# A gated delta rule with a rational-function layer: queries transposed on TensorE instead of through DRAM

## The chip, the core and the metric

The kernel runs on one core of a Trainium2 chip. The metric is the device time of one execution in microseconds. The engines are called as in the profile: PE (TensorE; PEld is its weight load), DVE (VectorE), ACT (ScalarE), POOL (GpSimd) and SP (SyncE, which here only issues transfers). All names of lines (L250 and so on) are those of the kernel before.

## What is computed

The reference has two stages. The first is a delta-rule attention over 4 batches of 8 heads, 768 steps and head size 48; the second a layer on each of the 3072 tokens (384 wide, 2048 hidden) whose activation is a rational function.

```python
k_n = k / (norm(k) + 1e-06)
for t in range(S):
    kt, vt, bt = k_n[:, :, t], v[:, :, t], beta[:, :, t, None]
    y[:, :, t] = einsum('bhd,bhde->bhe', q[:, :, t], state)
    v_old = einsum('bhde,bhd->bhe', state, kt)
    state = state + bt * einsum('bhd,bhe->bhde', kt, vt - v_old)
h = x @ w_in                       # x: y with the heads side by side
P = a[0] + a[1]*h + a[2]*h**2 + a[3]*h**3
Q = 1.0 + abs(b[0])*abs(h) + abs(b[1])*h**2
return (P / (Q + 1e-6)) @ w_out
```

All arrays are 32-bit floats. The kernel multiplies on PE in 16 bits: each operand is split into a high and a low 16-bit part, and three products (high-high, low-high, high-low) are summed in PSUM.

## The kernel before

**Chunks and units.** The 768 steps are cut into 12 chunks of 64. A chunk's tile has 128 partitions: 64 steps of two batches. In a chunk the recurrence is solved as a triangular system, so that it becomes matrix products. The layer runs in units: a unit is one of the 8 slices of the hidden size for the 256 tokens of one chunk, 96 units in all. A unit goes through `hidden` (the products with w_in, L851), `numerator` (L868 to L879), `quotient` (L886 to L898) and `accumulate` (the products with w_out, L913). In the numerator ACT's L868 and L870 come first and DVE's L871, L873 and L875 take their results together with PSUM. In the quotient DVE's L892 or L890, L893 and L897 work on operands that all lie in SBUF, and POOL makes the low part of the result at L898 (and, for some units, L879 and L895).

**How the two are interleaved.** A prologue (the string `ORDER`) loads and converts the weights (L382 to L394) and runs the first chunks' attention. After that, beside each unit of chunk c, one slice j of the attention's stages is issued: `back` for chunk c+1, `middle` for c+2, `front` for c+3 and `ahead` for c+4. Some stages are given a higher priority. A scheduler fixes the order of the instructions on each engine before the run; engines then work in that order and wait on one another by semaphores. Nearly all transfers are issued on SP's queue, also in a fixed order, so a transfer that waits holds back those behind it.

**The queries.** `load` (L112) fetches a chunk's queries in four transfers into one buffer, at the end of `ahead`. In `front`, slice 2, `scales` takes the sum of squares of the queries on ACT (L258), finds a power of two as scale by two small products on PE, and copies it out at L696 (tile sc). Then `queries_transposed` (L704) does this:

- POOL multiplies the queries by the scale in place (L261).
- `transposed` (L517) splits them on POOL into a high part (L242) and a low part (L248), both in the tile kn. That tile exists once and is also used for the keys in `keys_normalized`.
- Two transfers take kn to DRAM (L528, xdq).
- One transposing transfer brings the result back to SBUF as tq (L545). For chunk 0 only, PE transposes the 16-bit parts instead (L538) and ACT copies them out of PSUM (L540); its transfers to DRAM are issued all the same.

The tile tq has the head size on its partitions, two batches above each other with a pad from 48 to 64. It is read in `query_products` (L719), slice 3 of `front`, by the products pm (L470), which DVE masks at L725, and later in `diagonals` by the transfers to qbd (L502), which are needed for the chunk's outputs.

**The helpers.** `split16` (L239) is used everywhere for a split: by default ACT makes the high part (L244 without a scale, L246 with one) and DVE the low part (L248 without, L250 with a scale).

**PSUM.** The pool `ps_f` has one buffer of two banks (tag "a"). The products of `front` (pg, pm), the scale's two small products, `off_blocks` (pe) and, from chunk 3 on, the tokens' transposes (px, L819) take turns in it.

Of the kernel before, what the change touches and what calls it, by code (L numbers as in the profile page):

```python
# [10 lines left out]
F16 = mybir.dt.float16  # L11
F32 = mybir.dt.float32
# [26 lines left out]
def kernel(  # L39
# [12 lines left out]
    nc = tc.nc  # L52

    B, H, S, D = q.shape
    DM, DFF = moe_w_in.shape
    P = 128
    C = 64
    DP = 64
    NB = C // 16
    NCH = S // C  # L60
    NPAIR = B // 2
# [4 lines left out]
    HG = 2  # L66
# [39 lines left out]


    SRC = {"k": k, "q": q, "v": v}
    LD_BUFS = {"k": 1, "q": 1, "v": 2}
    loaded = {}  # L110

    def load(nm, c):  # L112
        t = sb.tile([P, NPAIR * H, D], F32, tag="ld" + nm, name=f"{nm}_{c}", bufs=LD_BUFS[nm])
        with behind(nm, c):
            for b in range(2):
                sl, src = slice(b * C, (b + 1) * C), SRC[nm][:, :, c * C : (c + 1) * C]
                if nm == "v":
                    nc.sync.dma_start(out=t[sl], in_=src[2 * b : 2 * b + 2].rearrange("p h t d -> t (p h) d"))
                else:
                    for i in range(2):  # L120
                        nc.sync.dma_start(out=t[sl, i * H : (i + 1) * H], in_=src[2 * i + b].rearrange("h t d -> t h d"))
        loaded[nm, c] = t


    identf = cpool.tile([P, P], F32, name="identf")
    make_identity(nc, identf)
# [130 lines left out]
    def sum_squares(dst, src, junk):  # L257
        nc.scalar.activation(junk, src, AF.Square, accum_out=dst)  # L258

    def scaled(x, scale):  # L260
        nc.gpsimd.tensor_scalar(x, x, scale, 0.0, op0=ALU.mult, op1=ALU.add)  # L261
# [255 lines left out]
    def transposed(x, src, nm, soon):  # L517


        split16(  # L520
            [x[:, i, :, :, :D].rearrange("p h b d -> p b h d") for i in range(2)],
            src.rearrange("p (b h) d -> p b h d", b=2),
            eng=nc.gpsimd,
            hi=nc.gpsimd,
        )
        xd = dpool.tile([NPAIR, 2, NH, C, HG, 2, DP], F16, tag="xd" + nm[0], name=f"xd{nm}", bufs=4 if nm[0] == "k" else 2)
        for p in PAIRS:
            nc.sync.dma_start(  # L528
                out=xd[p].rearrange("i n t a b d -> t (i n) (a b d)"),
                in_=x[p * C : (p + 1) * C].rearrange("t i (n a) b d -> t (i n) (a b d)", n=NH),  # L530
            )
        t = sb.tile([P, NPAIR, 2, NH, C, HG], F16, tag="tt", name="t" + nm)
        if soon:
            pts = ps_f.tile([P, 2, H, P], F16, tag="a", name=f"pt{nm}")
            for i in range(2):
                pt = pts[:, i]
                for h in range(H):
                    nc.tensor.transpose(pt[:, h], x[:, i, h].rearrange("p b d -> p (b d)"), ident16)  # L538
                for p in PAIRS:
                    nc.scalar.copy(  # L540
                        t[:, p, i].rearrange("x n t a -> x n a t"),
                        pt[:, :, p * C : (p + 1) * C].rearrange("x (n a) t -> x n a t", a=HG),
                    )
            return t, xd
        nc.sync.dma_start(  # L545
            out=t.rearrange("x p i n t a -> x (p i n t a)"),
            in_=xd.rearrange("p i n t a b d -> (p i n t a) (b d)"),
            transpose=True,
        )
        return t, xd  # L550
# [127 lines left out]
    def scales(c):  # L678

        qt, vs = loaded.pop(("q", c)), loaded.pop(("v", c))  # L680
        fs = sb.tile([P, 2], F32, tag="fs", name=f"fs_{c}")
        for i, t in enumerate((qt, vs)):
            junk = sb.tile([P, HP, D], F32, tag="fq", name=f"sq{i}_{c}", bufs=1)
            sum_squares(fs[:, i : i + 1], t, junk)
        if "v" in fmax:
            nc.gpsimd.tensor_scalar(fs[:, 1:2], fs[:, 1:2], fmax["v"], 1.0, op0=ALU.max, op1=ALU.mult)
        fmax["v"] = fs[:, 1:2]
        kq = sb.tile([P, 2], F32, tag="kq", name=f"kq_{c}")
        hot = sb.tile([P, 2], BF16, tag="hq", name=f"hq_{c}")
        key_of(kq, total(fs, 2, f"q_{c}"))  # L690
        found(hot, kq)
        pl = ps_f.tile([P, NPAIR * 512], F32, tag="a", name=f"pl_{c}")
        looked_up(pl[:, 0:2], hot[:, 0:1], t_qv[:, 0:2])
        looked_up(pl[:, 2:5], hot[:, 1:2], t_qv[:, 2:5])
        sc = sb.tile([P, 6], F32, tag="sc", name=f"sc_{c}", bufs=4)
        nc.scalar.copy(sc[:, 0:5], pl[:, 0:5])  # L696
        nc.scalar.activation(sc[:, 5:6], sc[:, 1:2], AF.Copy, scale=sc[:, 3:4])
        d = info[c]
        d["sq"], d["sv"], d["isv"], d["ss"], d["iy"] = (sc[:, i : i + 1] for i in (0, 2, 3, 4, 5))
        d["qt"], d["vs"] = qt, vs  # L700
        if c == 0:
            scaled(vs, d["sv"])

    def queries_transposed(c):  # L704
        d = info[c]
        qt = d.pop("qt")
        scaled(qt, d["sq"])
        d["tq"] = transposed(kn_b, qt, f"q_{c}", c == 0)[0]

    def diagonals(c):  # L710
        d = info[c]
# [379 lines left out]
```

## Time and profile before

| | before |
|---|---|
| median of 3 runs | 859.67 us (859.34 to 860.39) |
| the profiled execution's own time | 859.42 us |
| its span, first to last instruction | 857.2 us |
| mean granted TensorE clock | 0.886 |
| HBM read, written | 40.47 MB, 26.23 MB |

The profile shows one execution. Its rows give, for a group of instructions, the line, engine and operation, what it writes and reads ("out<-in" by the program's names), shapes and count, then busy time in us and the mean of one in ns, and after the second bar the idle time of the engine just before them and what ended it. A row of waits ("POOL x <- DMA y: 23.0, 7, 5.2") gives the us in total, the number of times and the longest. A row of the chain of waits gives start and duration in us. In the rows of one line or tile, three numbers with strokes are the shortest, the median and the longest duration in ns.

### The profile page before, as it was taken

The page shows a single profiled execution, that of the slowest core. Times are in us where ns is not written, and L with a number is a line of the kernel's source. Part 1 is how long each engine was busy: PE and PEld are TensorE (multiplying, and loading weights), DVE is VectorE, ACT ScalarE, POOL GpSimd, SP SyncE. Part 2 cuts the span into 40 slices and gives each one's busy share as a digit, 9 for nine tenths or more (in the row PEclk, how much of TensorE's full clock was granted, in tenths as well). Part 3 has the DMA queues.
Part 4 walks back from the last instruction along what each step waited for, and adds up shares of the span by engine and source line. Part 5 has one row for each costly group of instructions (what it writes and reads, how often), then busy time and mean ns, then how long its engine had stood idle before and what let it go on. Part 6 is the DMA issues. An engine that isn't in the chain of part 4 may idle for free.

```text
span 857.2 us, 22995 instructions
## 1 busy us (share of the span) xinstructions
PE 622.0 (73%) x9290; PEld 492.0 (57%) x9290; DVE 760.8 (89%) x1312; ACT 544.9 (64%) x980; POOL 482.7 (56%) x452
## 2 busy tenths in 40 slices
PE   0220344766878688878798697995987989999895
PEld 0220344546666475666586585774775767777663
DVE  5998799697989969989989968999789999898996
ACT  4766656645666465677586574766566766677774
POOL 7655666355326437646736864766665635454532
PEclk9755555897988989989999899998989999999999
DMA  8996868898787875965997988598778672500000
GB/s 235 247 205 132 191 160 152 152 159 152 141 142 130 154 147 89 176 116 104 186 151 132 151 137 173 90 167 150 123 151 153 94 151 47 102 2 20 1 20 19
DMA packets 466506, 111.46 MB, mean 130 GB/s; under 512 B 431328, under 2 KB 463072, under 8 KB 466400
## 3 DMA queue, kind: packets, MB, share of 16 engines
q1 hardware_dynamic: 464224, 108.83, 67.8%
q8 instruction: 73, 1.20, 0.6%
q10 hardware_dynamic: 2176, 1.17, 0.5%
q14 instruction: 33, 0.27, 0.1%
HBM read 40.47 MB, written 26.23 MB: 78 GB/s over the span
## 4 chain that ended last, share of the span: by engine, by line
DVE 40%; DMA 16%; PE 14%; ACT 9%; issue 9%; SPq 7%; POOL 4%; POOLq 0%; ACTq 0%; DVEq 0%
PE ph L851 4%; PE po L913 4%; DVE mw L893 4%; DVE mw L873 3%; DVE mu L871 3%; DVE mg L892 3%; DVE mu L897 3%; DVE w_out L394 3%; DVE pr L636 2%; DVE mu L875 2%; DMA gd<-g 2%; DMA gb<-gd 2%; SPq L676 2%; POOL mg L898 2%; DMA wc<-img 1%
## 5 line engine op out<-in xcount | busy, mean ns | idle before, releaser
L913 PE MATMUL po<-w_out,mg 128*128 128x384 f16 x1152 | 224.9, 341 | 50.5 <-POOL mg L898 43.0
L851 PE MATMUL ph<-xT,w_in 128*128 128x256 f16 x1728 | 216.6, 278 | 13.1 <-DVE mu L875 11.4
L898 POOL TENSOR_TENSOR mg<-mu,mr 128x512 f16<-128x512 f32 x96 | 134.1, 1398 | 115.0 <-DVE mu L897 85.3
L851 PEld LDWEIGHTS <-w_in 128*128 128x128 f16 x1728 | 169.2, 100 | 45.5 <-issue 12.5
L913 PEld LDWEIGHTS <-mg 128*128 128x128 f16 x1152 | 110.2, 101 | 126.5 <-POOL mg L898 51.3
L868 ACT ACTIVATE mu<-ph,coef,msc 128x512 f32<-128x512 f32 x96 | 74.0, 771 | 45.5 <-POOL mg L898 31.0
L874 ACT ACTIVATE mw<-mw 128x512 f32<-128x512 f32 x96 | 60.3, 628 | 64.4 <-DVE mw L873 64.1
L893 DVE SCALAR_TENSOR_TENSOR mw<-mw,msc,mg 128x512 f32<-128x512 f32 x96 | 96.1, 1002 | 0.5
L470 PEld LDWEIGHTS <-kbd 128*128 128x128 f16 x1680 | 61.9, 105 | 36.4 <-issue 27.8
L871 DVE TENSOR_TENSOR mu<-ph,mu 128x512 f32<-128x512 f32 x96 | 65.4, 681 | 19.1 <-ACT mr L870 16.5
L875 DVE SCALAR_TENSOR_TENSOR mu<-mu,msc,ph 128x512 f32<-128x512 f32 x96 | 70.7, 736 | 0.0
L873 DVE SCALAR_TENSOR_TENSOR mw<-mr,msc,ph 128x512 f32<-128x512 f32 x96 | 70.5, 735 | 0.0
L886 ACT ACTIVATE mr<-mw,msc 128x512 f32<-128x512 f32 x96 | 69.2, 720 | 1.5
L895 POOL TENSOR_TENSOR mu<-mu,mw 128x512 f32<-128x512 f32 x36 | 48.7, 1353 | 32.8 <-DVE mw L893 29.1
L870 ACT ACTIVATE mr<-ph,msc 128x512 f32<-128x512 f32 x96 | 65.3, 680 | 0.0
L470 PE MATMUL pu<-z,ebd 128*128 128x48 f16 x1728 | 53.3, 187 | 15.7 <-DVE z L250 14.2
L470 PEld LDWEIGHTS <-ebd 128*128 128x128 f16 x1728 | 52.6, 99 | 19.5 <-issue 16.8
L887 ACT ACTIVATE mr<-mr 128x512 f32<-128x512 f32 x96 | 60.3, 628 | 1.4
L892 DVE SCALAR_TENSOR_TENSOR mg<-mu,msc,mr 128x512 f16<-128x512 f32 x60 | 56.9, 949 | 4.3 <-ACT mr L887 4.3
L879 POOL TENSOR_SCALAR mu<-mu,msc 128x512 f32<-128x512 f32 x36 | 34.2, 949 | 38.8 <-DVE mu L875 38.7
L897 DVE SCALAR_TENSOR_TENSOR mu<-mu,msc,mw 128x512 f32<-128x512 f32 x60 | 54.3, 907 | 0.4
L470 PEld LDWEIGHTS <-wbd 128*128 128x128 f16 x1152 | 35.1, 99 | 33.9 <-issue 30.4
(211 smaller groups left out, 1247.8 us busy)
## 6 DMA issues: line engine op xcount, KB each, us to landing
wsi<-in_moe_w_in_dram SPq DMA_DIRECT2D x24, 256.0 KB, 5.2
xdk<-kn SPq DMA_DIRECT2D x24, 256.0 KB, 3.9
kbd<-tk SPq DMA_DIRECT2D x24, 256.0 KB, 4.5
gd<-g SPq DMA_DIRECT2D x24, 256.0 KB, 4.3
wso<-in_moe_w_out_dram SPq DMA_DIRECT2D x32, 192.0 KB, 4.3
xdq<-kn SPq DMA_DIRECT2D x24, 256.0 KB, 4.3
mbd<-mm SPq DMA_DIRECT2D x24, 256.0 KB, 5.0
wc<-img SPq DMA_DIRECT2D x24, 256.0 KB, 5.1
```

The costliest lines, as they stand in the source:

```text
L470: nc.tensor.matmul(dst[p][:, h], head(bd, lp, p * H + h), head(rt, rp, p * H + h), start=start and n == 0 and h == 0, stop=stop and n == l ...
L851: nc.tensor.matmul(ph[:, i], w_in[:, f2, wp, cc, i * P : (i + 1) * P], x[:, xp, cc], start=k == 0, stop=k == 3 * NCC - 1,)
L868: nc.scalar.activation(u, ph, AF.Identity, scale=A3, bias=a2)
L871: nc.vector.tensor_mul(u, ph, u)
L873: nc.vector.scalar_tensor_tensor(out=w, in0=z, scalar=B0, in1=ph, op0=ALU.add, op1=ALU.mult)
L875: nc.vector.scalar_tensor_tensor(out=u, in0=u, scalar=A1, in1=ph, op0=ALU.add, op1=ALU.mult)
L886: nc.scalar.activation(r, w, AF.Ln, bias=Q0)
L892: nc.vector.scalar_tensor_tensor(out=g[:, 0], in0=u, scalar=A0, in1=r, op0=ALU.add, op1=ALU.mult)
L893: nc.vector.scalar_tensor_tensor(out=w, in0=w, scalar=Q0, in1=g[:, 0], op0=ALU.add, op1=ALU.mult)
L897: nc.vector.scalar_tensor_tensor(out=u, in0=u, scalar=A0, in1=w, op0=ALU.add, op1=ALU.subtract)
L898: nc.gpsimd.tensor_mul(g[:, 1], u, r)
L913: nc.tensor.matmul(po[p], g[:, gp, i, p * P : (p + 1) * P], w_out[:, f2, wp, i], start=f2 == lo and i == 0 and k == 0, stop=f2 == hi - 1 a ...
```

## The change

Queries are loaded into a tile of their own, `q_b`, which exists once and keeps each head's two batches side by side with the pad of 16 zeros that the transposed form needs. The zeros are written once at the start. The queries stay unscaled in 32 bits there. `queries_transposed` then issues 16 PE transposes of 64 x 128 words in 32 bits, one for each half of the partitions and each head, into one tile pt of the pool `ps_f`; a transpose's 64 columns are written with a step of two words, because the head index within a pair is innermost. From there `split16` writes tq: ACT makes the high part from PSUM with the scale (L246), DVE the low part (L250). The POOL instructions on the queries, the tile kn's use by the queries, the transfers xdq and the transposing transfers to tq are gone, and so is the special way of chunk 0. The sum of squares reads the padded tile without its pad. The last part of the diff makes the scratch space for descriptors that software writes smaller, which leaves the room in SBUF for the larger tile.

```diff
-    LD_BUFS = {"k": 1, "q": 1, "v": 2}
+    LD_BUFS = {"k": 1, "v": 2}
...
     def load(nm, c):
-        t = sb.tile([P, NPAIR * H, D], F32, tag="ld" + nm, name=f"{nm}_{c}", bufs=LD_BUFS[nm])
+        if nm == "q":
+            t = q_b
+        else:
+            t = sb.tile([P, NPAIR * H, D], F32, tag="ld" + nm, name=f"{nm}_{c}", bufs=LD_BUFS[nm])
...
                     for i in range(2):
+                        if nm == "q":
+                            nc.sync.dma_start(out=t[sl, :, i, :D], in_=src[2 * i + b].rearrange("h t d -> t h d"))
+                            continue
                         nc.sync.dma_start(out=t[sl, i * H : (i + 1) * H], in_=src[2 * i + b].rearrange("h t d -> t h d"))
...
+    q_b = cpool.tile([P, H, 2, DP], F32, name="q_b")
+    nc.vector.memset(q_b[..., D:], 0.0)
...
-            sum_squares(fs[:, i : i + 1], t, junk)
+            sum_squares(fs[:, i : i + 1], t if i else t[..., :D].rearrange("x h b d -> x (h b) d"), junk)
...
     def queries_transposed(c):
         d = info[c]
         qt = d.pop("qt")
-        scaled(qt, d["sq"])
-        d["tq"] = transposed(kn_b, qt, f"q_{c}", c == 0)[0]
+        t = d["tq"] = sb.tile([P, NPAIR, 2, NH, C, HG], F16, tag="tt", name=f"tq_{c}")
+        pt = ps_f.tile([P, NPAIR, NH, C, HG], F32, tag="a", name=f"ptq_{c}")
+        for p in PAIRS:
+            sl = slice(p * C, (p + 1) * C)
+            for h in range(H):
+                nc.tensor.transpose(
+                    pt[:, p, h // HG, :, h % HG], qt[sl, h].rearrange("x b d -> x (b d)"), identf[sl, sl]
+                )
+        split16([t[:, :, i].rearrange("x p n t a -> x p (n t a)") for i in range(2)], pt.rearrange("x p n t a -> x p (n t a)"), d["sq"])
...
-    nc = _bacc.Bacc("TRN2", target_bir_lowering=False, num_devices=1)
+    nc = _bacc.Bacc("TRN2", target_bir_lowering=False, num_devices=1, dynamic_dma_scratch_size=1024)
```

## The prediction

> **What bounds the kernel now.** The first view is the busy table of the page, which gives each engine's share of the whole span. The second is the table by stage. I cut it at 162 us, where the rational-function units have begun, and at 700 us, where the last queries have gone to DRAM.
>
> ```profile
> PE 622.0 (73%) x9290; PEld 492.0 (57%) x9290; DVE 760.8 (89%) x1312; ACT 544.9 (64%) x980; POOL 482.7 (56%) x452
> 162.00:700.00 538.00, 433.52 (x6883) 344.30 (x6880) 485.78 (x751) 340.31 (x567) 312.89 (x256) 0.93 0.79 140
> 700.00:820.00 120.00, 111.00 (x1457) 86.47 (x1455) 109.99 (x156) 87.45 (x140) 60.24 (x47) 1.00 0.20 38
> ```
>
> In the stage rows the columns are the stage's length, then PE, PEld, DVE, ACT and POOL busy, the granted clock, the DMA share and GB/s. DVE is the fullest engine: it is idle in 538 - 485.78 = 52.2 us of the middle stage, 9.7%. After 700 us hardly any attention DMA is left (DMA share 0.20 against 0.79), and DVE is still idle in 10.01 of 120 us, 8.3%. So most of DVE's idle time is the hand-over between engines inside the units. Waits peculiar to the attention's transfers can be worth about (9.7% - 8.3%) of 538 us, 7.4 us.
>
> The third view is the chain of waits.
>
> ```profile
> DVE 40%; DMA 16%; PE 14%; ACT 9%; issue 9%; SPq 7%; POOL 4%; POOLq 0%; ACTq 0%; DVEq 0%
> 124.91 3.62 DMA xdq<-kn
> 227.47 3.25 DMA xdq<-kn
> 474.03 4.47 DMA tq<-xdq
> 524.75 4.41 DMA tq<-xdq
> 582.33 3.70 DMA xdq<-kn
> ```
>
> The chain runs through the queries' two transfers five times, 19.5 us in all. That would be the gain if nothing else were late. But DVE is nearly full at the same time, so the chain cannot be read as a saving by itself. The waits say who really stood:
>
> ```profile
> POOL kn L242 <- DMA xdq<-kn: 23.0, 7, 5.2
> PE pm L470 <- DMA tq<-xdq: 16.2, 7, 4.7
> L725 DVE TENSOR_TENSOR m<-pm,mask 128x1024 f32<-128x1024 f32 x12 | 14.6, 1215 | 4.3 <-PE pm L470 4.3
> ```
>
> POOL lost 23.0 us because the keys' split (L242) shares one buffer, kn, with the queries and had to let xdq out of it first. PE lost 16.2 us at the query products. Of all this only 4.3 us can be read off DVE directly, before the masking at L725.
>
> **What the change adds to DVE: +15.4 us.** Each of the 12 chunks gets one new scalar_tensor_tensor, PSUM plus one 16-bit SBUF input, 128x1024. The same line already does this at 768 elements, and L873 does a like one at 512.
>
> ```profile
> L250 DVE SCALAR_TENSOR_TENSOR z<-pu,zmask,z x36: 998/1006/1020, 106.1 to 768.1; 128x768 f16<-128x768 f32 x36
> L873 DVE SCALAR_TENSOR_TENSOR mw<-mr,msc,ph x96: 726/735/741, 154.0 to 843.0; 128x512 f32<-128x512 f32 x96
> L893 DVE SCALAR_TENSOR_TENSOR mw<-mw,msc,mg x96: 658/747/2201, 165.8 to 847.4; 128x512 f32<-128x512 f32 x96
> ```
>
> The three figures are shortest, median and longest. From 512 to 768 elements the median grows by 271 ns, so 1024 take 1006 + 271 = 1277 ns, and 12 of them 15.3 us; with L725's 1215 ns as the lower bound it is 14.6 us. The lines of these three tiles also show something else. L250 on PSUM and L873 on PSUM scatter by 22 and 15 ns, L893, whose inputs are both in SBUF, by a factor of three. The new instruction reads PSUM and so should keep its length. The pad of the new query tile is cleared once at the start, 128x256 words like the pad of kn:
>
> ```profile
> L197 POOL MEMSET kn<- x1: 312/312/312, 2.5 to 2.5; 128x256 f32 x1
> ```
>
> On DVE that costs between 0 and 0.3 us; I take 0.1, and 15.4 us together. All of it is on the fullest engine, so I count it in full.
>
> **What it takes off POOL, and so off DVE: -15.9 us.** The three POOL instructions of each chunk go:
>
> ```profile
> L248 POOL TENSOR_TENSOR kn<-q,kn 128x768 f16<-128x768 f32 x12 | 21.8, 1813 | 0.4
> L261 POOL TENSOR_SCALAR q<-q,sc 128x768 f32<-128x768 f32 x12 | 14.1, 1173 | 7.8 <-ACT sc L696 5.9 <-DMA wc<-img 1.6
> L242 POOL TENSOR_SCALAR kn<-q 128x768 f16<-128x768 f32 x12 | 12.4, 1034 | 0.8
> ```
>
> That is 48.3 us of an engine with idle time, by itself worth nothing. But the scatter of L893 comes from it: where such a DVE instruction meets a POOL instruction, it does not end before that one does. The timeline of both engines at 459 us, and at the last chunk:
>
> ```profile
> 459.11 2.09 POOL L248 TENSOR_TENSOR kn<-q,kn 128x768 f16<-128x768 f32 x1
> 459.73 2.02 DVE L897 SCALAR_TENSOR_TENSOR mu<-mu,msc,mw 128x512 f32<-128x512 f32 x1
> 685.72 1.67 POOL L248 TENSOR_TENSOR kn<-q,kn 128x768 f16<-128x768 f32 x1
> 685.83 1.58 DVE L619 TENSOR_TENSOR pr<-wt,ab 128x4 f32<-128x4 f32 x1
> 687.64 0.17 DVE L619 TENSOR_TENSOR pr<-wt,ab 128x16 f32<-128x16 f32 x1
> ```
>
> L897 is L893's twin in shape and takes 2.02 us here in place of some 0.75. L619 takes 1.58 us for four elements under the POOL instruction, and 0.17 us for sixteen once that is over. I took, for every DVE instruction of the trace, the excess over the shortest fifth of its own line and shape, and divided it over the POOL instructions that lay beside it by the time they overlapped. In all, DVE loses 127.7 us in this way, 17% of its busy time. The three query lines carry 15.9 us of it, in 31 DVE instructions. The first is an L394 of the weights under the scaling at 39.49, the last the L619 just shown:
>
> ```profile
> 38.74 1.37 DVE L394 SCALAR_TENSOR_TENSOR w_out<-wsi,w_out 128x256 uint32<-128x256 uint32 x2
> 39.49 1.31 POOL L261 TENSOR_SCALAR q<-q,sc 128x768 f32<-128x768 f32 x1
> ```
>
> The other bound is the plain rate: 48.3 of POOL's 482.7 us are 10.0%, and 10.0% of 127.7 is 12.8 us. It would be nothing if the POOL instructions behind moved up into the same places. I take 15.9, since it is counted on the very instructions that go, and keep 12.8 and 0 for the range.
>
> **Stalls that go: -6 us.** The kn buffer is no longer shared, so POOL's 23.0 us go; tq no longer comes by DMA, so PE's 16.2 us go. DVE's own share lies between the 4.3 us before L725 and the 7.4 us of the stage comparison; I take 6. Next in line behind the stalls is DVE itself. SP's queue also gets shorter, which I take to be inside these 6 us:
>
> ```profile
> L528 SPq DMA_DIRECT2D xdq<-kn x24: 601/658/2616, 55.8 to 691.0; - x24
> L545 SPq DMA_TRANSPOSE tq<-xdq x11: 1942/2309/3907, 130.4 to 702.6; - x11
> q1 hardware_dynamic: 464224, 108.83, 67.8%
> ```
>
> 24 issues of 0.66 us and 11 of 2.31 us make 41 us of SP time. The transfers move 24 x 256 KB and 11 x 512 KB, some 12 of the 108.8 MB. The four loads of q per chunk stay where they are in the queue and now wait for the last transpose in place of POOL's L248, a few us earlier.
>
> **New waits: +3.5 us.** The query's way is now PE, ACT, DVE, PE. The transposes wait for the PSUM buffer that the scale's lookup leaves, and behind them on PE stand the units' products; ACT's split waits for the transposes, and behind it stand the units' L868 and L870, for which DVE waits at L871; DVE's half waits for ACT's, with L871 behind it; the products pm wait for DVE's half. DVE already has such pairs:
>
> ```profile
> DVE z L250 <- ACT z L246: 7.2, 4, 4.2
> DVE xT L250 <- ACT xT L246: 5.8, 5, 2.2
> DVE et L250 <- ACT et L246: 4.7, 3, 2.5
> ```
>
> 17.7 us over 36 + 12 + 12 pairs are 0.30 us each, 3.5 us for 12 new ones; from z alone 2.4, from xT alone 5.8.
>
> **PE and ACT: nothing, net.** PE gets 16 transposes per chunk; six of 128x128 in 32 bits take 0.82 us in the timeline, so 16 take some 2.2 us, 26 us in all. ACT gets 12 instructions of 1018 ns, as L586 from PSUM, and loses four copies of the first chunk.
>
> ```profile
> 798.30 0.82 PE L819 MATMUL px<-identf,y 128*128 128x128 f32 x6
> L819 PE MATMUL px<-identf,y 128*128 128x128 f32 x72 | 11.4, 301 | 2.0 <-ACT sf L812 1.6 <-ACT sf L815 0.3
> L586 ACT ACTIVATE g<-pg 128x1024 f32<-128x1024 f32 x12 | 12.2, 1018 | 9.3 <-PE pg L470 9.3
> L540 ACT COPY tq<-ptq 128x512 f16<-128x512 f16 x4 | 2.6, 718 | 0.0
> ```
>
> On PE the 16.2 us of standing before pm and the first chunk's 16 transposes in 16 bits go against the 26 us; the cover for the rest is PE's idle fifth of the middle stage. Without it PE would cost up to 10 us. ACT's 12.2 - 2.6 us lie in its idle third. The smaller descriptor scratch gives nothing: the queues listed hold no transfers of POOL.
>
> No instruction of this trace writes PSUM with a step of two words, as the new transposes do (the head index lies innermost). The Trainium skill, "PSUM — Partial Sum Buffer", section "Specifications (TRN2)", says that any access that is not contiguous slows matmuls significantly, since PSUM's lines are 8 bytes. That speaks against this change; it gives no figure, and it is weighed as the last of the rivals.
>
> **The sum.** The profiled execution took 859.42 us, its span 857.2 and 2.2 around it; the median of the runs is 859.67, so the two can be used alike. 859.4 + 15.4 - 15.9 - 6 + 3.5 = 856.4 us. Runs of before lie within 0.2% of one another, 1.7 us, which is about what can be told from no change.
>
> **Rivals.**
> *The split is paid in full.* POOL's queue closes up: with three instructions fewer, the units' L898 and L895 start earlier and stand before the same DVE instructions as often as the queries' did. Then nothing of the 15.9 us returns: 859.4 + 15.4 - 6 + 3.5 = 872.3, slower. For it speaks that POOL's other lines carry the remaining 111.8 us of DVE's stretching; against it, that POOL's total load falls. It decides at 12.9 us: if less of the contention than that returns, the kernel is slower than before. Chance 0.27.
> *The path through DRAM was the bound.* All five pieces of the chain go: 859.4 + 15.4 - 15.9 - 19.5 + 3.5 = 842.9. For it speak the chain and SP, against it the 8.3% idle of a stage without these transfers. Chance 0.18.
> *Give and take.* Contention falls by the rate only: 859.4 + 15.4 - 12.8 - 6 + 3.5 = 859.5, no change. Chance 0.16.
> *The transposes crawl.* If the stepped writes keep the transposes from overlapping, each takes L819's mean of 301 ns in place of 137: 192 x 0.164 = 31.5 us more on PE. PE is on 14% of the chain, so 4.4 us of that count, 860.8 us; counted in full 888. This is the mechanism by which the skill's rule would show. No row here speaks for or against it. Chance 0.07, mostly slower.
>
> **How the numbers follow.** My forecast has 0.32: between 849 and 857.7. With the second rival that makes faster 0.50; same is 0.16; slower 0.27 + 0.07 = 0.34. The time is the forecast's 856.4. The second rival's 842.9 and the first's 872.3 are the far ends of their cases (every piece of the chain, none of the contention), so the range, 842 to 873, takes in both; it leaves out the transposes that count in full and whatever an order of instructions that came out better or worse on the whole would add, which I put at under 2 in 10. The forecast's own range is 853 (14.6 in place of 15.4, 7.4 in place of 6, 2.4 in place of 3.5) to 859.
>
> **What would show it.** Right: a DVE group of 12 at L250 of about 1.28 us each, without scatter; no POOL line on q; DVE's busy time within 3 us of 760.8, because L893, L897, L892 and L619 have lower means; no row of POOL waiting for xdq and none of PE waiting for tq; DVE idle near 8.3% in the middle stage. Wrong: L893's mean still near its 1.0 us, with DVE's busy time up by 10 us or more (first rival); a span shorter by over 10 us with DVE's idle time well under 8% (second); transposes of 300 ns from start to start (last); or a new long wait of ACT or DVE at the split, or of PE at pm, which would make the term of 3.5 us wrong.

## The result, and the profile after

| | before | after |
|---|---|---|
| median, same chip (4 runs each) | 859.58 us (859.34 to 860.39) | 832.08 us (829.89 to 833.35) |
| ratio to before | 1 | 0.9681, 95% interval 0.9656 to 0.9707 |
| profiled execution | 859.42 us | 831.25 us |
| its span | 857.2 us | 829.5 us |
| DVE busy; span less busy | 760.8; 96.4 us | 752.7; 76.8 us |
| stretching of DVE beside POOL, summed as in the prediction | 127.7 us | 104.4 us |

The change makes the kernel 3.2% faster. The direction was forecast, the size was not: 832.1 us lies 24 us below the forecast and 10 us below the range. The span fell by 27.7 us, 8.1 in DVE's busy time (760.8 - 752.7) and 19.6 in its idle time (96.4 - 76.8). The lines of code have moved: L250, L246 and L893 of before are L259, L255 and L909 here; L868, L870 and L871 are L884, L886 and L887; L913 is L929, L470 is L479, and the transposes are L721.

The page after, its busy table, its main DMA queue (packets, MB, share of the 16 engines) and its chain of waits by engine:

```profile
PE 626.5 (76%) x9466; PEld 498.2 (60%) x9466; DVE 752.7 (91%) x1325; ACT 553.8 (67%) x988; POOL 428.0 (52%) x416
...
q1 hardware_dynamic: 428672, 96.77, 63.0%
...
DVE 44%; PE 16%; issue 11%; DMA 11%; ACT 7%; SPq 6%; POOL 5%; POOLq 0%; DVEq 0%; ACTq 0%
```

POOL lost 54.7 us and DVE 8.1 although it has 13 instructions more. 12.06 MB of transfers are gone, and DMA's part of the chain fell from 16% to 11%. The table by stage after, with the columns of the prediction's, in the same two stages:

```profile
162.00:700.00 538.00, 454.32 (x7333) 363.75 (x7330) 498.09 (x787) 362.90 (x594) 277.55 (x229) 0.96 0.70 121
700.00:820.00 120.00, 109.56 (x1193) 82.07 (x1188) 109.52 (x156) 88.08 (x143) 50.26 (x41) 1.00 0.13 26
```

DVE is idle in 538 - 498.09 = 39.9 us of the middle stage, 7.4%, where it was 52.2 us. In the tail it is 10.5 of 120 us, 8.7%. The middle stage is now fuller than the tail, which the prediction had taken for a floor.

The new tile's rows after (shortest, median and longest in ns), and the row of the DVE group that the prediction watched for contention:

```profile
L255 ACT ACTIVATE tq<-ptq,sc x12: 1093/1108/1138, 40.3 to 658.3; 128x1024 f16<-128x1024 f32 x12
L259 DVE SCALAR_TENSOR_TENSOR tq<-ptq,sc,tq x12: 1268/1272/1277, 42.3 to 660.0; 128x1024 f16<-128x1024 f32 x12
```

```profile
L909 DVE SCALAR_TENSOR_TENSOR mw<-mw,msc,mg 128x512 f32<-128x512 f32 x96 | 89.9, 937 | 0.6
```

And the same group in the kernel before, whose shortest, median and longest instruction the prediction showed:

```profile
L893 DVE SCALAR_TENSOR_TENSOR mw<-mw,msc,mg 128x512 f32<-128x512 f32 x96 | 96.1, 1002 | 0.5
```

The split costs 12 times 1.272, 15.3 us, and scatters by 9 ns. The mean of the group of 96 has come down from 1002 to 937 ns. The transposes of the first and of the third chunk in the timeline of PE, with six of the tokens' transposes (L835, which was L819) for comparison, and the rows of waits that bear on the new path:

```profile
37.16 1.60 PE L721 MATMUL ptq<-identf,q_b 64*128 64x64 f32 x16 [2.73 <-ACT sc L705]
164.86 1.02 PE L721 MATMUL ptq<-identf,q_b 64*128 64x64 f32 x16 [0.26 <-ACT sc L705]
345.90 0.82 PE L835 MATMUL px<-identf,y 128*128 128x128 f32 x6
```

```profile
ACT sq L267 <- DMA q_b<-in_q_dram: 19.7, 7, 7.3
PE ptq L721 <- ACT sc L705: 3.6, 3, 2.7
DVE z L259 <- ACT z L255: 2.9, 4, 1.2
DVE xT L259 <- ACT xT L255: 1.3, 1, 1.3
ACT tq L255 <- PE ptq L721: 1.2, 2, 0.8
DVE et L259 <- ACT et L255: 0.8, 1, 0.8
PE pm L479 <- DVE tq L259: 0.5, 1, 0.5
```

Sixteen transposes take 1.60 us in the first chunk and 1.02 us in the third. Each writes 64 columns with a step of two words; each of the tokens' six writes 128 columns without a step. There is no row of DVE waiting for ACT at tq; the three pairs that cost 17.7 us before cost 2.9 + 1.3 + 0.8 = 5.0 now. POOL's wait for xdq and PE's for the transfer to tq have no row any more. ACT's wait for the loads of the queries before their sum of squares grew from 14.3 to 19.7 us; it was this in the kernel before:

```profile
ACT sq L258 <- DMA q<-in_q_dram: 14.3, 5, 5.1
```

### The profile page after: what moved, and what is told of

It is laid out like the page before. It is cut to its first block, busy times and chain, and to the rows that moved or that the text cites. A ratio compares the mean times of both kernels' runs of the same rounds, so it can differ in the third digit from the quotient of the medians.

```text
span 829.5 us, 23311 instructions
## 1 busy us (share of the span) xinstructions
PE 626.5 (76%) x9466; PEld 498.2 (60%) x9466; DVE 752.7 (91%) x1325; ACT 553.8 (67%) x988; POOL 428.0 (52%) x416
## 4 chain that ended last, share of the span: by engine, by line
DVE 44%; PE 16%; issue 11%; DMA 11%; ACT 7%; SPq 6%; POOL 5%; POOLq 0%; DVEq 0%; ACTq 0%
PE ph L867 6%; PE po L929 5%; DVE mw L909 4%; DVE mu L887 4%; DVE mw L889 4%; DVE mu L891 4%; DVE w_out L403 4%; DVE mg L908 3%; DMA q_b<-in_q_dram 3%; DVE mu L913 2%; POOL mg L914 2%; PE pu L479 1%; DVE mg L906 1%; ACT mu L884 1%; DVE z L259 1%
## 5 line engine op out<-in xcount | busy, mean ns | idle before, releaser
L867 PE MATMUL ph<-xT,w_in 128*128 128x256 f16 x1728 | 222.4, 280 | 20.5 <-DVE mu L891 16.7
L929 PE MATMUL po<-w_out,mg 128*128 128x384 f16 x1152 | 218.5, 333 | 24.2 <-POOL mg L914 22.2
L914 POOL TENSOR_TENSOR mg<-mu,mr 128x512 f16<-128x512 f32 x96 | 132.3, 1378 | 154.4 <-DVE mu L913 99.2
L929 PEld LDWEIGHTS <-mg 128*128 128x128 f16 x1152 | 108.6, 100 | 93.6 <-POOL mg L914 29.8
L884 ACT ACTIVATE mu<-ph,coef,msc 128x512 f32<-128x512 f32 x96 | 73.9, 770 | 33.5 <-PE ph L867 19.7
L909 DVE SCALAR_TENSOR_TENSOR mw<-mw,msc,mg 128x512 f32<-128x512 f32 x96 | 89.9, 937 | 0.6
L887 DVE TENSOR_TENSOR mu<-ph,mu 128x512 f32<-128x512 f32 x96 | 65.4, 681 | 24.2 <-ACT mr L886 13.3
L479 PEld LDWEIGHTS <-kbd 128*128 128x128 f16 x1680 | 60.7, 104 | 26.7 <-issue 15.1
L886 ACT ACTIVATE mr<-ph,msc 128x512 f32<-128x512 f32 x96 | 65.2, 679 | 0.0
L479 PE MATMUL pu<-z,ebd 128*128 128x48 f16 x1728 | 51.5, 185 | 15.5 <-DVE z L259 13.7
L479 PEld LDWEIGHTS <-ebd 128*128 128x128 f16 x1728 | 50.8, 98 | 18.9 <-issue 15.5
L479 PEld LDWEIGHTS <-wbd 128*128 128x128 f16 x1152 | 33.9, 99 | 29.1 <-issue 28.5
L895 POOL TENSOR_SCALAR mu<-mu,msc 128x512 f32<-128x512 f32 x36 | 30.9, 858 | 36.9 <-DVE mu L891 34.8
L913 DVE SCALAR_TENSOR_TENSOR mu<-mu,msc,mw 128x512 f32<-128x512 f32 x60 | 49.2, 820 | 0.4
```

Source lines behind the costliest of these rows:

```text
L479: nc.tensor.matmul(dst[p][:, h], head(bd, lp, p * H + h), head(rt, rp, p * H + h), start=start and n == 0 and h == 0, stop=stop and n == l ...
L867: nc.tensor.matmul(ph[:, i], w_in[:, f2, wp, cc, i * P : (i + 1) * P], x[:, xp, cc], start=k == 0, stop=k == 3 * NCC - 1,)
L884: nc.scalar.activation(u, ph, AF.Identity, scale=A3, bias=a2)
L887: nc.vector.tensor_mul(u, ph, u)
L909: nc.vector.scalar_tensor_tensor(out=w, in0=w, scalar=Q0, in1=g[:, 0], op0=ALU.add, op1=ALU.mult)
L913: nc.vector.scalar_tensor_tensor(out=u, in0=u, scalar=A0, in1=w, op0=ALU.add, op1=ALU.subtract)
```

## The experiments

My first theory after the result: the gain is two things, POOL's work no longer stretching DVE, and the transfers no longer making DVE wait, each larger than forecast. The rivals: one of the two alone is the cause; the shared tile kn was the price; or the order of the instructions, which the scheduler draws anew for every edit, happened to come out better. Ratios are to the kernel before on the same chip, where its median was 854.1 to 856.6 us, with 95% intervals.

**POOL's work put back into the kernel after.** It writes two tiles that nobody reads; the transfers stay away.

```diff
+        qx = sb.tile([P, HP, D], F32, tag="qx", name=f"qx_{c}", bufs=1)
+        kx = sb.tile([P, 2, HP, D], F16, tag="kx", name=f"kx_{c}", bufs=1)
+        nc.gpsimd.tensor_scalar(qx, qt[..., :D].rearrange("x h b d -> x (h b) d"), d["sq"], 0.0, op0=ALU.mult, op1=ALU.add)
+        split16([kx[:, i] for i in range(2)], qx, eng=nc.gpsimd, hi=nc.gpsimd)
```

> The changed kernel with three extra POOL instructions per chunk that do the queries' old work (scaling, high part, low part, same sizes) from the query tile into tiles that nobody reads: 48 us of POOL work comes back, no transfer, no consumer. Theory A (the gain beyond the forecast is POOL's work: DVE instructions with two SBUF inputs stand behind POOL instructions, and the units' own POOL work queues behind the queries'): DVE's busy time rises again by 16 to 23 us, its idle time by 5 or so, and the time is 850 to 857. Theory B (the transfers through DRAM, their issue on SP and their waits were the cost): 832 to 836, since none comes back. Theory C (the order of instructions was drawn anew, and came out better): anything from 825 to 860, with no match between DVE's busy time and the added POOL work.

0.9913 (0.989 to 0.9936). Its busy table, and its rows of the added tile:

```profile
PE 632.6 (75%) x9466; PEld 501.0 (59%) x9466; DVE 765.6 (91%) x1325; ACT 553.5 (66%) x988; POOL 476.5 (56%) x452
```

```profile
L727 POOL TENSOR_SCALAR qx<-q_b,sc x12: 898/1031/1425, 39.0 to 669.6; 128x768 f32<-128x768 f32 x12
L251 POOL TENSOR_SCALAR kx<-qx x12: 822/1236/1497, 41.2 to 670.7; 128x768 f16<-128x768 f32 x12
L257 POOL TENSOR_TENSOR kx<-qx,kx x12: 1639/1652/2090, 45.6 to 674.1; 128x768 f16<-128x768 f32 x12
...
who waited for it (us, times):
```

The list of those who waited for it is empty, and still 2.3% of the time comes back. DVE's busy time rises by 765.6 - 752.7 = 12.9 us, less than the 16 expected, with the same 1325 instructions, and its stretching from 104.4 to 121.0. Contention with POOL is a cause by itself; a second order below repeats it.

**The transfers put back into the kernel after.** They carry a tile of zeros to DRAM and a transposed copy to a tile that nobody reads; POOL's work stays away.

```diff
+    kx = cpool.tile([P, 2, H, 2, DP], F16, name="kx")
+    nc.gpsimd.memset(kx.bitcast(F32), 0.0)
...
+        xd = dpool.tile([NPAIR, 2, NH, C, HG, 2, DP], F16, tag="xdq", name=f"xdq_{c}", bufs=2)
+        for p in PAIRS:
+            nc.sync.dma_start(
+                out=xd[p].rearrange("i n t a b d -> t (i n) (a b d)"),
+                in_=kx[p * C : (p + 1) * C].rearrange("t i (n a) b d -> t (i n) (a b d)", n=NH),
+            )
+        if c > 0:
+            tx = sb.tile([P, NPAIR, 2, NH, C, HG], F16, tag="tx", name=f"tx_{c}", bufs=1)
+            nc.sync.dma_start(
+                out=tx.rearrange("x p i n t a -> x (p i n t a)"),
+                in_=xd.rearrange("p i n t a b d -> (p i n t a) (b d)"),
+                transpose=True,
+            )
```

> The changed kernel with the queries' old transfers added at their old place: two transfers of 256 KB to DRAM per chunk and, from chunk 1 on, one transposing transfer back, from a tile of zeros into a tile that nobody reads. SP gets its 41 us of issues back and the queues their 12 MB; nobody waits for the results and POOL gets nothing. Theory A: 832 to 836. Theory B in the form that SP's queue and the load on the DMA engines are the cost: 842 to 852, with longer landings and DVE idle up by 10 us or more. If the transfers cost only through those who waited for them (POOL at the keys' split, PE at the products), also 832 to 836, which the kernel with a buffer of its own for the queries' split tells apart.

0.9942 (0.992 to 0.9963). Its busy table and its middle stage, then where the added transfers are issued on SP's queue (the last two numbers with "to" are the first and the last start):

```profile
PE 631.4 (74%) x9466; PEld 501.3 (59%) x9466; DVE 744.6 (88%) x1325; ACT 552.0 (65%) x988; POOL 432.6 (51%) x417
```

```profile
162.00:700.00 538.00, 451.15 (x7249) 361.27 (x7247) 479.66 (x768) 351.85 (x583) 272.12 (x221) 0.93 0.77 138
```

```profile
L729 SPq DMA_DIRECT2D xdq<-kx x24: 596/903/1127, 9.3 to 274.5; - x24
L735 SPq DMA_TRANSPOSE tx<-xdq x11: 1699/3397/5452, 43.6 to 310.5; - x11
```

Nobody needs these transfers, and 2.6% of the time comes back. DVE's busy time does not rise; its idle time does, to 850.7 - 744.6 = 106.1 us in all and 58.3 in the middle stage. But they are not the old transfers in their old places. Being free of dependences, all of them are issued by 311 us, where the kernel before issues its own from 55.8 to 702.6 us. The rows of the two stretches before and behind 320 us, first of the kernel after, then of this one:

```profile
0.00:320.00 320.00, 180.75 (x2872) 148.81 (x2873) 286.10 (x632) 197.01 (x410) 160.06 (x199) 0.82 0.80 160
320.00:700.00 380.00, 333.20 (x5399) 265.93 (x5396) 355.28 (x538) 267.67 (x434) 215.82 (x176) 0.97 0.68 118
```

```profile
0.00:320.00 320.00, 169.31 (x2613) 135.94 (x2614) 260.60 (x597) 184.69 (x388) 150.18 (x192) 0.79 0.94 187
320.00:700.00 380.00, 331.13 (x5348) 266.73 (x5345) 349.74 (x541) 262.44 (x434) 213.33 (x174) 0.96 0.70 125
```

In the first 320 us, where they are crowded and the DMA share rises from 0.80 to 0.94, DVE is idle 25.5 us longer (286.10 - 260.60). From 320 to 700 us it is idle 5.5 us longer, within what other orders of the kernel after show below. So unread transfers cost by being there, in the stretch in which they run. What the old transfers cost in their old places this does not show.

**A tile of their own for the queries' 16-bit parts**, in the kernel before; all the rest stays.

```diff
+    knq_b = zeroed(1, [P, 2, H, 2, DP], F16, "knq", lambda t: t[:, :, :, :, D:DP])[0]
...
-        d["tq"] = transposed(kn_b, qt, f"q_{c}", c == 0)[0]
+        d["tq"] = transposed(knq_b, qt, f"q_{c}", c == 0)[0]
```

(With the smaller descriptor scratch, for room.)

> The kernel before with one change: the queries are split into a 16-bit tile of their own, so that POOL's split of the keys no longer waits until the queries' transfer has left the shared tile (23.0 us of POOL standing); the descriptor scratch is made smaller to fit it. Everything else, the transfers and POOL's work on the queries, stays. If the shared tile's wait is a large part of the gain: 846 to 852. If POOL's work itself (theory A) or the transfers (theory B) are it: 856 to 860.

1.0223 (1.0196 to 1.0249), slower. POOL's row of 23.0 us behind xdq is gone altogether, and this row stands in the waits:

```profile
PE pm L471 <- DMA tq<-xdq: 26.2, 8, 5.5
```

Taking away the largest named stall of the prediction's list gained nothing in this kernel, which is one order of its instructions. PE's wait for tq grew from 16.2 to 26.2 us instead.

**Transposes on PE in 16 bits for every chunk**, in the kernel before: the transfers go, POOL's work stays, and ACT gets four copies from PSUM in each chunk.

```diff
-        for p in PAIRS:
+        for p in PAIRS if nm[0] == "k" else ():
...
-        d["tq"] = transposed(kn_b, qt, f"q_{c}", c == 0)[0]
+        d["tq"] = transposed(kn_b, qt, f"q_{c}", True)[0]
```

(Also the smaller scratch.)

> The kernel before with the way of its first chunk for all chunks: POOL scales and splits the queries as before, PE transposes the two 16-bit parts (32 transposes... 16 per chunk) and ACT copies them out of PSUM in four copies of 0.72 us per chunk; the queries' transfers to DRAM and back are left out. POOL's 48 us stay, DVE gets nothing, ACT gets 2.9 us per chunk, 32 us in all. Theory A: the contention stays and ACT is fuller, 855 to 862. Theory B: the transfers and both waits are gone, 840 to 850.

0.9953 (0.9933 to 0.9973). Its busy table:

```profile
PE 634.5 (75%) x9466; PEld 501.0 (59%) x9466; DVE 753.6 (89%) x1312; ACT 568.3 (67%) x1024; POOL 476.5 (56%) x452
```

Stretching is 123.0 us, as POOL's work is there. But idle time is 847.7 - 753.6 = 94.1 us, hardly less than before, with no transfer of the queries left. Taking the transfers away is not enough by itself when the work lands on ACT (23.4 us more) behind POOL, in the one order that was run.

**Tiny forms of both**, in the kernel after: POOL's three instructions on one column in place of 768 (the same diff with `qt[:, 0, 0, :1]`), and the same number of transfers with 2 KB in place of 256 KB each, the transposing one on 16 rows.

> The changed kernel with the three extra POOL instructions per chunk of the first experiment, at the same place and with the same dependences, but one column wide: 36 instructions of some 0.2 to 0.3 us in place of 48 us. Theory A (the first experiment lost its time to POOL's work): the same ratio to before as the changed kernel, 0.965 to 0.972. Theory C (any edit draws the order on the engines anew, and the first experiment's loss was the draw): 0.98 to 1.0, with POOL's work as low as in the changed kernel.

> The changed kernel with the added transfers of the second experiment, as many and at the same place, but 2 KB each and a transposing transfer of 4 KB: SP's issues stay in number, the 12 MB go. If the bytes were the second experiment's loss: ratio 0.965 to 0.972. If SP's issues were: 0.98 to 0.99. Theory C: anything in 0.96 to 1.0 without a match.

0.9559 (0.953 to 0.9588) and 0.9714 (0.9689 to 0.9739). The tiny transfers leave the kernel where it was, so the number of transfers is not what costs. Their issues on SP's queue:

```profile
L729 SPq DMA_DIRECT2D xdq<-kx x24: 278/306/1162, 9.3 to 78.8; - x24
L732 SPq DMA_TRANSPOSE tx<-xdq x11: 1085/1198/2792, 37.1 to 179.5; - x11
```

These issues are also about three times shorter at the median than those of the large transfers (0.306 against 0.903 us, 1.198 against 3.397). Whether the bytes or SP's time cost is therefore not told apart. The tiny POOL instructions make the kernel faster than the kernel after, which no theory of mine says; stretching is 99.3 us with as many POOL instructions as before (452).

**Other orders.** One call, `queries_transposed`, is moved from slice 2 to slice 3 of `front`, in four kernels: after, before, and the two with something put back.

> The changed kernel with queries_transposed called one slot later (slot 3 of front, just ahead of the products that need it). The instructions are the same ones in number, size and dependences; only the order on the engines is drawn anew. If the order hardly matters: ratio to before 0.965 to 0.972. Theory C: it moves by 1 to 3%, with DVE's stretching and POOL's work about the same and DVE's idle time different.

> The kernel before with queries_transposed called one slot later, as in the run beside it. Same instructions, another order. If the order hardly matters: ratio 0.997 to 1.003. Theory C: off by 1 to 3% either way; if it comes out faster, part of the change's gain was a bad draw of before.

> The first experiment (POOL's old work on the queries added to the changed kernel, into tiles that nobody reads) with queries_transposed called one slot later, which draws another order on all engines. If POOL's work costs what the trace counted on the instructions that went (16 us of stretched DVE instructions): DVE's stretching 118 to 124 us again, DVE's busy time 764 to 768, ratio to before 0.985 to 1.0. If the first experiment's loss was a bad order: ratio 0.96 to 0.98 this time.

> The second experiment (the queries' old transfers added to the changed kernel, nobody waits for them) in another order, by the same edit. If 12 MB through the same queue cost DVE idle time whoever waits: DVE idle about 100 us again, stretching below 106, ratio 0.985 to 1.0. If it was the order: DVE idle 70 to 80, ratio 0.96 to 0.98.

After 0.9762 (0.9721 to 0.9802); POOL's work back 0.9945 (0.9921 to 0.9968); the transfers back 0.9978 (0.9955 to 1.0001). In the kernel before the instructions came out in the same order on every engine, so its 1.0014 (0.9988 to 1.0039) is a repeat. **Both put back**, and the kernel before with the one-column POOL instructions as one more order of it:

> The changed kernel with both added: POOL's old work on the queries and their old transfers, none of it used. All that is left of the change is that PE, ACT and DVE make the transposed queries and that nobody waits for POOL and the transfers on their account. If both costs are real and add up: DVE's stretching near 122, DVE idle near 105, ratio 1.0 to 1.025, since DVE pays its 15.3 us for nothing. If the two overlap or the gain lay in the waits alone: 0.97 to 0.99.

> The kernel before with three POOL instructions of one column added per chunk, which draws another order of the same work (the call one slot later gave the very same order, so that run told nothing of orders). If orders scatter by 1% and before was an ordinary draw: ratio 0.99 to 1.015, DVE's stretching about 128 and its idle time 90 to 107. If before was a bad draw and the change mostly got a better one: 0.97 to 0.985.

1.0112 (1.0078 to 1.0146) and 1.0013 (0.9992 to 1.0035). With both back the kernel after is slower than before, by about 1%. It then has POOL's work, the transfers (all of them in the first 289 us) and the new split's 15.3 us; its idle time is 90.9 us, below the 105 expected. The other kernel has the smaller descriptor scratch too, as have the kernel before with tiny transfers (1.0098, below) and the change itself; neither is faster than before, so the scratch is not the gain.

**POOL's part alone, with the real transfers.** In the kernel before ACT scales the queries and makes the high part, and DVE makes the low part, in SBUF; kn, xdq and tq stay as they were.

```diff
+        on = nc.gpsimd if nm[0] == "k" else None
         split16(
...
-            eng=nc.gpsimd,
-            hi=nc.gpsimd,
+            eng=on,
+            hi=on,
...
-        scaled(qt, d["sq"])
+        nc.scalar.activation(qt, qt, AF.Copy, scale=d["sq"])
```

> The change's POOL part alone, with the transfers and their waits as in the kernel before: of the queries, ACT does the scaling and the high part and DVE the low part, all in SBUF (12 DVE instructions more of some 0.8 to 1.1 us, 24 on ACT). If the time of before was lost mainly in the contention with POOL, this comes to about 0.985 to 0.995 of before (DVE busy lower by 5 to 10 us). If it was lost mainly in DVE's waits behind the path through DRAM, DVE's idle time stays at some 95 us and the time at 0.995 to 1.01. If the two have to go together, the same: about 1.00.

0.9829 (0.9787 to 0.9871). Its busy table, its DVE group of the split (busy, mean ns), and its waits on the two old transfers:

```profile
PE 622.4 (74%) x9290; PEld 492.8 (59%) x9290; DVE 754.9 (90%) x1324; ACT 561.0 (67%) x1004; POOL 440.4 (52%) x416
```

```profile
L248 DVE TENSOR_TENSOR kn<-q,kn 128x768 f16<-128x768 f32 x12 | 11.6, 970 | 0.0
```

```profile
POOL kn L242 <- DMA xdq<-kn: 18.6, 5, 5.4
PE pm L470 <- DMA tq<-xdq: 18.1, 7, 4.8
```

About half of the gain is there, and both named waits stand nearly as they were (18.6 and 18.1 us). DVE pays 11.6 us for the split and is stretched by 17.0 us less (110.7). Its idle time is 840.8 - 754.9 = 85.9 us, 10.5 less than before, although every transfer is there.

**How much is order.** The kernel after and the one with one-column POOL instructions once more, together on one chip, and the kernel before with the tiny transfers added.

> The kernel after, unchanged, on the same chip as the next one: 0.965 to 0.971 of before if the ratio does not hang on the chip.

> The kernel after with three one-column POOL instructions per chunk, a second time: 0.953 to 0.960 if it is the order of the instructions that makes it faster than the kernel after, 0.965 to 0.971 if the first time it was the chip.

> The kernel before with the same tiny transfers beside its own, which draws another order of its instructions. If the gain of the change is not the luck of one order, this stays within 0.995 to 1.01 and DVE's idle time within 90 to 107 us; if orders of the kernel before scatter as widely as the gain, it can come to 0.975 or below with DVE idle under 85 us.

0.9704 (0.9666 to 0.9742), 0.9553 (0.9521 to 0.9586) and 1.0098 (1.0061 to 1.0134). The busy tables of the first two:

```profile
PE 626.2 (76%) x9466; PEld 498.9 (60%) x9466; DVE 752.5 (91%) x1325; ACT 554.5 (67%) x988; POOL 432.7 (52%) x416
```

```profile
PE 620.4 (76%) x9466; PEld 494.3 (61%) x9466; DVE 744.9 (91%) x1325; ACT 551.8 (68%) x988; POOL 442.7 (54%) x452
```

The second does everything the first does and 36 small instructions more, and is 12.5 us faster (817.63 us, 815.85 to 819.41, against 830.14, 828.96 to 831.69). The longest sequence of DVE instructions (by operation, tiles and shape) that both have in the same order holds 64% of them. It is the fastest kernel of this study. Its advantage over the kernel after repeats, and I know no work that it saves; that its order is the cause is an inference.

**All kernels together.** A single pair of kernels differs by the edit and by the order. Over all of them the two can be told apart better. "Old" is the way on which the queries are split into 16-bit parts in SBUF and transposed from there, by transfers or in 16 bits on PE; "new" is the way of the change, in 32 bits through PE. Stretching and idle time (span less busy) are of DVE, in us. The two columns of idle time by stretch are cut at 320 us, behind the last of the unread transfers. The cut was chosen with the traces at hand.

| kernel | way used | POOL's query work | queries' transfers | stretching | idle | idle, 0 to 320 | idle, 320 to 700 | ratio |
|---|---|---|---|---|---|---|---|---|
| before | old | yes | yes | 127.7 | 96.4 | 46.3 | 31.9 | 1 |
| own tile for the queries' parts | old | yes | yes | 128.9 | 106.9 | 41.1 | 49.1 | 1.022 |
| before, tiny POOL work added | old | yes | yes | 122.6 | 98.4 | 40.3 | 39.3 | 1.001 |
| before, tiny transfers added | old | yes | yes | 122.5 | 103.5 | 47.8 | 39.0 | 1.010 |
| POOL's part alone | old | no | yes | 110.7 | 85.9 | 30.7 | 36.6 | 0.983 |
| 16-bit transposes on PE | old | yes | no | 123.0 | 94.1 | 36.5 | 40.0 | 0.995 |
| both put back | new | yes | unread | 124.4 | 90.9 | 53.7 | 20.6 | 1.011 |
| transfers put back | new | no | unread | 95.3 | 106.1 | 59.4 | 30.3 | 0.994 |
| transfers put back, moved | new | no | unread | 102.0 | 98.1 | 53.9 | 25.8 | 0.998 |
| POOL's work put back | new | yes | no | 121.0 | 78.4 | 39.2 | 23.0 | 0.991 |
| POOL's work put back, moved | new | yes | no | 119.1 | 84.6 | 48.6 | 19.6 | 0.995 |
| after | new | no | no | 104.4 | 76.8 | 33.9 | 24.7 | 0.968 |
| after, again | new | no | no | 103.9 | 75.2 | 31.9 | 25.1 | 0.970 |
| after, moved | new | no | no | 104.1 | 77.8 | 29.0 | 31.3 | 0.976 |
| after, tiny transfers added | new | no | tiny | 105.7 | 73.9 | 35.0 | 23.6 | 0.971 |
| after, tiny POOL work added | new | tiny | no | 99.3 | 68.8 | 29.1 | 24.2 | 0.956 |
| the same, again | new | tiny | no | 100.5 | 70.8 | 30.0 | 26.7 | 0.955 |

These are the rows of the kernel before for the two stretches:

```profile
0.00:320.00 320.00, 168.76 (x2582) 136.59 (x2583) 273.66 (x593) 185.97 (x392) 173.37 (x204) 0.77 0.84 166
320.00:700.00 380.00, 315.68 (x5071) 251.26 (x5070) 348.07 (x525) 249.72 (x415) 238.54 (x195) 0.95 0.77 139
```

Stretching follows POOL's work, whatever the order: 119.1 to 128.9 us in the eight rows with it, mean 123.7, and 95.3 to 110.7 in the nine without, mean 102.9 (36 tiny instructions count as none).

Idle time as a whole follows no single column. In the first 320 us it follows POOL's work too, where no unread transfers lie: 36.5 to 48.6 us in the seven rows with that work, 29.0 to 35.0 in the seven without. Unread transfers bring it to 53.7 and more. From 320 to 700 us it follows the way that is used: 31.9 to 49.1 us in the six rows of the old way, mean 39.3, and 19.6 to 31.3 in the eleven of the new, mean 25.0, whatever unread work lies beside it. The 16-bit transposes, which have no transfers of the queries, stand with the old way there (40.0).

The ratio of kernels with the same or nearly the same work scatters by about 2%: 0.955 to 0.976 like after, 1.000 to 1.022 like before. The 3.2% is thus larger than what order does within a kind, and every order of the one kind is faster than every order of the other.

## Why the prediction was wrong in size

**The split, +15.4 us: right.** 15.3 for the twelve, and 0.27 for clearing the pad. It keeps its length beside POOL, as argued from L250 and L873. "The split is paid in full" fell: more of the contention returned than the 12.9 us at which that rival was to be decided.

**Contention, -15.9 us: right in kind, too small.** Between the two kernels stretching fell by 23.3 us, and between the two groups of the table by 123.7 - 102.9 = 20.8. The bound of 12.8 by the rate, and the case of give and take with it, were too low. The 15.9 counted only the instructions that lay beside the query lines. POOL's work put back gave 16.6 and, both kernels moved, 119.1 - 104.1 = 15.0, near it. Where the rest of the 23.3 comes from is not shown; kernels without the work differ by up to 15 us in stretching (95.3 to 110.7). The Trainium skill, "SBUF — State Buffer", section "Who interferes with whom", says that a VectorE instruction with two inputs in SBUF contends with a GpSimd instruction that reads SBUF. The runs agree as far as they go: 36 POOL instructions of one column add nothing to the stretching, and 36 of 768 columns add 16.6 and 15.0 us.

**Stalls, -6 us, and new waits, +3.5 us: the step that failed.** The prediction said: "DVE's own share lies between the 4.3 us before L725 and the 7.4 us of the stage comparison; I take 6." DVE's idle time fell by 19.6 us between the two kernels, where -2.5 had been forecast. Two errors are in it. The bound of 7.4 us took the tail's idle share, 8.3%, for the least that the middle stage could have. After the change the middle stage has 7.4% while the tail has 8.7%. A likely reason, which no run here tests, is that DVE has other chunks' work to fill a gap with in the middle stage and only the last units in the tail. And the comparison began at 162 us, although the first 162 us hold 7.3 us of the 19.6 (143.28 - 135.95), as this stage's rows of before and of after show, in this order:

```profile
0.00:162.00 162.00, 50.92 (x773) 43.55 (x774) 135.95 (x366) 95.39 (x239) 99.02 (x142) 0.65 0.85 188
```

```profile
0.00:162.00 162.00, 59.63 (x939) 50.98 (x940) 143.28 (x383) 101.78 (x250) 98.34 (x146) 0.73 0.87 190
```

With the cut at 320 us, 12.4 of the 19.6 lie ahead of it (46.3 - 33.9) and 7.2 behind it (31.9 - 24.7). Ahead of it the runs put the loss to POOL's work on the queries, whose 48.3 us the prediction had called "by itself worth nothing" apart from the stretching: all rows with that work are above all rows without it, unless unread transfers lie there. Behind it they put it to the use of the old way: by the means of the two groups 14.3 us (39.3 - 25.0), twice the bound of 7.4.

The new waits did not come: DVE never stands behind ACT at tq, and its other pairs of the kind cost 5.0 us where they had cost 17.7.

With the measured terms the sum is 859.4 + 15.3 - 23.3 - 19.6 = 831.8, against 831.25 for the profiled execution. That it comes out proves no cause, since busy and idle time make up the span.

**The named waits do not give the price.** I had sized the stalls from rows of waits. In the kernel with its own tile POOL's 23.0 us went, and it was slower, in one order. In the kernel with POOL's part alone 18.6 and 18.1 us of these waits stayed, and half of the gain came; the idle time from 320 to 700 us stayed too (36.6). "The path through DRAM was the bound" came nearest with 842.9, its 19.5 us is close to the 19.6 that idle time lost, and its sign came: a span shorter by over 10 us, with DVE idle 7.4% of the middle stage. But it is not shown to be right. Over half of the 19.6 lies in the first 320 us, where the rows follow POOL's work, and the old way without the transfers through DRAM (the 16-bit transposes) keeps DVE as idle from there to 700 us as the others of that way.

**The transposes crawl: wrong.** The rule of the Trainium skill, "PSUM — Partial Sum Buffer", section "Specifications (TRN2)", that access that is not contiguous slows matmuls, weighed in the prediction as a rival, shows in no row here. Sixteen transposes that write 64 columns with a step of two words took 1.02 us in the third chunk, 0.064 us each; six that write 128 columns without a step took 0.82, 0.137 each. By the column that is about the same. The prediction's 2.2 us for sixteen had counted 128 columns. PE and ACT in sum cost nothing visible, as forecast.

**What stays open.** Which piece of the old way empties DVE by some 14 us from 320 to 700 us is not settled. The wait at the shared tile was taken away in one kernel, the transfers and with them the wait for tq in another, and DVE's idle time there was 49.1 and 40.0 us. Why POOL's work on the queries leaves DVE idle in the first 320 us is not settled either. For the unread transfers a later landing of other transfers may be the reason: the loads of the weights to the tile wsi took 5.6 us to land at the median, against 4.8 in the kernel after. No run here isolates it. And of the 27.5 us between the two medians, a part can be the luck of an order: kernels of nearly the same work lie up to 2.2% apart, some 19 us.

## What to carry to other kernels

Do not take the idle share of one stage as the floor of another; the tail of a pipeline may have less work to fill its gaps with. Do not price a transfer by the rows of those who wait for it. When it is put back unread to see what it costs, look first where the scheduler has placed it: without dependences it moves to the front, and what it costs there is not what it cost in its old place. Where a scheduler draws a new order for each edit, judge an edit over several orders, by the engine's stretching and by its idle time in each stretch, before one pair's ratio is believed.

## What was not expected of the hardware

Work that nobody reads costs time too. POOL's unread instructions (47 us of them by their medians, 12 times 1.031 + 1.236 + 1.652 us) took the kernel after from 0.968 to 0.991 of before, and its moved form from 0.976 to 0.995, though POOL, busy 52% there, is idle nearly half of the time. Transfers that bring zeros to an unread tile took the same two to 0.994 and 0.998, with the loss mostly in the first 320 us, where they ran. And PSUM written with a step of two words did not slow the 32-bit transposes visibly (0.064 us for 64 columns, 0.137 for 128 without a step).
